# More short products at the start, a new written order of steps, and a split last store in an attention and maxout kernel

## The chip, the cores and the metric

One core of one Trainium2 chip. The metric is the time of one execution on the device in microseconds (us), shown as the median of several runs.

## What is computed

Windowed attention is followed by a maxout feed-forward layer:

```python
scores = scale * np.matmul(q, k.transpose(0, 1, 3, 2))      # 8 batches, 8 heads, 576 positions, 64 wide
attn = softmax(np.where(masks, scores, -1e9))               # window of 32; heads 4 to 7: 128, every 4th position
x = np.matmul(attn, v)                                      # 4608 tokens x 512
h = np.maximum(np.maximum(x @ w1, x @ w2), x @ w3)          # 768 wide
out = h @ w_out                                             # 4608 x 512
```

All data are 32-bit floats. A product of 32-bit operands is made as three products of operands split into a high and a low part.

## The kernel before

Heads are taken two at a time, so a batch has four pairs. The first eight pairs (`early`, L601) are done one by one with small products: scores (L641 adds the mask by an identity product, L649 multiplies q and k), maximum, subtraction, exponential, sum, reciprocal, scaling and a transpose on DVE, ACT and POOL, and then the values (L760). The result of a pair is copied from PSUM as a high part and as a remainder into `xs` (L456, L488); it is one of the four chunks that the first up products (`ups`, L1542) sum over. Tokens go through the layer in tiles of 512, 512, 768, 768, 1024 and 1024. The first two (`plain`, L1534) use plain products of 512 columns (L1551, down products L1490). The four later ones (`fast`, L1625) use a scheme of seven products on sums of blocks (L1793), with sums of the weights that are written to DRAM early (`sums_of`, L1104, stores L1145) and streamed back (L1753); their down products are L1357 (`turned_down`, L1241), whose results leave by `store` (L1376).

Each weight block (`weight`, L512) is loaded (L569), taken apart by ACT (L549), POOL or DVE (L554) and DVE (L560), copied (L456) and its remainder is formed (L488). The 18 blocks of up weights are numbered 0 to 17; step 6j is the load of block j.

Every piece of work is a step of a `Plan` (L275) with a number. The step says what it does and what it depends on, but the order is written out by hand: `SEQUENCE` (L60) lists all step numbers, and `issue` (L311) issues them in this order; each engine therefore runs its own steps in the order of the list and waits at each for what it needs. A letter behind a number (`382d`) names another engine than the step's first choice (a ACT, d DVE, p POOL). `f` is a filler (L2015): one unread bf16 product of 512 columns that only keeps PE busy. Ahead of the list, `issue` calls `short` (L2024) `SHORT` times: an unread product of 32 columns on a 32x32 corner. The first 36 loads are also held back so that no more than 2 million bytes are on their way at once (`gate`, L325).

Numbers that the prediction uses: loads of q and k 152 (pair 2), 170 (pair 0), 188 and 189 (pair 1), 207 (pair 3); loads of v 153, 171, 190, 208 for pairs 2, 0, 1, 3; scores 154, 172, 191, 209 and values 163, 181, 200, 218 for pairs 2, 0, 1, 3; 199 is the transpose for 200; 168 is one copy of pair 2's result; 182, 184, 186 copy pair 0's; 21 and 22 are the DVE and the ACT step of weight block 3; 366, 367, 382, 383 form sums of weight blocks (`both`, L1114).

Of the kernel before, what the change touches and what calls it, by code (L numbers as in the profile page):

```python
# [55 lines left out]
SHORT = 10  # L56
# [278 lines left out]
def tile_dilated_window_attention__then__maxout_ffn(  # L335
# [905 lines left out]
    def turned_down(t0, done, n, hf, load):  # L1241
# [147 lines left out]
        def copied(name, tag, bank, st):  # L1389
            t = buf(tag, name)  # L1390
            return t, plan.add(
                {"act": act(n), "dve": dve(n)}, lambda e: copy(e, t.t[:, :n], bank.t[:, :n]), [st], [bank, t]
            )
# [707 lines left out]
```

## Time and profile before

| | us |
|---|---|
| median of 3 runs | 629.5 (627.93 to 630.55) |
| profiled execution | 629.65 |
| its span, first to last instruction | 627.9 |
| PE busy | 618.7 (99%) |
| DVE busy | 499.4 (80%) |
| ACT busy | 311.9 (50%) |
| POOL busy | 203.0 (32%) |

PE multiplies, DVE, ACT and POOL work on vectors, SP issues loads and stores. The profile's own execution took 1.75 us more than its span. Busy times include the pipeline of a product, so a busy PE need not be PE at its peak; fillers count as busy.

### The profile page before, as it was taken

Reading aid. Unit: us, or ns where it says so; the run is one execution under the profiler, and the core shown is the slowest. Engines: PE = TensorE matmul, PEld = TensorE weight load, DVE = VectorE, ACT = ScalarE, POOL = GpSimd, SP = SyncE. Lnnn points to the kernel's source line nnn. Section 1 sums busy time; section 2 is a strip of 40 time slices with the busy share of each in tenths; the row PEclk is TensorE's granted clock in tenths of the full one; section 3 lists DMA queues with packets and bytes.
Section 4 is the critical chain, followed back from the end, with each engine's and each line's share of the span. In section 5 each row is a group of like instructions: output and inputs, shape, how many; then the busy total and the mean of one; then the engine's idle time right before and its main releaser. Section 6 shows DMA issues by size and latency. Waiting matters only on the chain.

```text
span 627.9 us, 16042 instructions
## 1 busy us (share of the span) xinstructions
PE 618.7 (99%) x6023; PEld 530.4 (84%) x6023; DVE 499.4 (80%) x1385; ACT 311.9 (50%) x932; POOL 203.0 (32%) x252
## 2 busy tenths in 40 slices
PE   9899999999999999999999999999999999999997
PEld 4577887888889999999999999887888888888886
DVE  6878798998899899999989899887759962335665
ACT  3445568575677464776245467822215522122243
POOL 3767988899857512212103010120000000000000
PEclk9899999999999999999999999999999999999999
DMA  7989948987698998878878966477457256757524
GB/s 276 307 282 339 405 149 290 320 286 247 226 348 262 304 301 294 306 253 277 285 244 261 325 226 219 142 230 250 135 184 248 92 170 222 237 178 235 175 84 151
DMA packets 79709, 153.23 MB, mean 244 GB/s; under 512 B 7952, under 2 KB 26384, under 8 KB 79632
## 3 DMA queue, kind: packets, MB, share of 16 engines
q1 hardware_dynamic: 79488, 151.94, 72.0%
q8 instruction: 48, 0.79, 0.5%
q14 instruction: 29, 0.24, 0.1%
q10 hardware_dynamic: 144, 0.26, 0.1%
HBM read 123.08 MB, written 29.10 MB: 242 GB/s over the span
## 4 chain that ended last, share of the span: by engine, by line
PE 88%; DMA 6%; DVE 3%; POOL 1%; ACT 1%; issue 1%; SPq 0%; DVEq 0%; ACTq 0%
PE ffn L1793 47%; PE ffn L1357 16%; PE ffn L1551 13%; PE ffn L1490 3%; PE pair L922 3%; PE pair L1082 3%; PE ffn L2016 1%; DMA kept_up<-hf 1%; DMA wup_a<-kept_up 1%; DMA fk<-in_qk_d_dram 1%; DMA hf<-in_fv_d_dram 1%; DMA kept_d<-dc 1%; DMA st<-in_w_up_dram 1%; DVE hf L488 1%; PE pair L760 1%
## 5 line engine op out<-in xcount | busy, mean ns | idle before, releaser
L1793 PE MATMUL ffn<-wup_a 128*128 128x384 f32 (+1 forms) x1188 | 235.6, 356 | 0.6 <-ACT u L456 0.4
L1793 PEld LDWEIGHTS ffn<-wup_a 128*128 128x128 f32 x1188 | 211.7, 188 | 19.5 <-issue 0.7
L1551 PE MATMUL ffn<-xs,wup_a 128*128 128x512 f32 x408 | 96.7, 394 | 1.5 <-DVE hf L488 1.1
L1551 PEld LDWEIGHTS ffn<-xs,wup_a 128*128 128x128 f32 x408 | 75.6, 188 | 18.6 <-issue 1.5
L488 DVE TENSOR_TENSOR hf<-ffn,hf 128x512 f32<-128x512 f32 (+1 forms) x96 | 60.9, 636 | 36.6 <-PE ffn L1793 33.8
L1026 DVE STREAM_TRANSPOSE PT<-W 32x256 f32<-32x256 f32 (+2 forms) x192 | 76.9, 401 | 4.1 <-POOL sm L996 0.4
L972 ACT ACTIVATE W<-W,mx 128x96 f32<-128x96 f32 (+2 forms) x180 | 65.7, 367 | 10.2 <-DVE mx L960 9.9
L456 ACT CAST hs_all<-hf 128x384 fp32r<-128x384 f32 (+4 forms) x57 | 32.8, 582 | 36.8 <-PE ffn L1357 18.1
L996 POOL TENSOR_SCALAR sm<-sm 128x8 f32<-128x8 f32 (+2 forms) x48 | 11.2, 233 | 121.0 <-ACT W L972 81.2
L456 ACT COPY ffn<-ffn 128x384 f32<-128x384 f32 (+1 forms) x31 | 16.0, 517 | 67.3 <-DVE hf L488 38.7
L1357 PE MATMUL ffn<-hs_all,wdn 128*128 128x512 f32 (+1 forms) x228 | 48.8, 363 | 0.0
L1793 PE MATMUL ffn<-wup_a,wdn 128*128 128x512 f32 x192 | 45.9, 390 | 0.0
L1357 PEld LDWEIGHTS ffn<-hs_all,wdn 128*128 128x128 f32 x228 | 41.3, 188 | 4.8
L456 ACT COPY u<-ffn 128x384 f32<-128x384 f32 (+1 forms) x34 | 18.0, 529 | 52.5 <-PE ffn L1793 46.6
L488 POOL TENSOR_TENSOR W<-W,sm 128x768 f32<-128x768 f32 (+2 forms) x33 | 34.6, 1051 | 25.4 <-DVE sm L1001 24.2
L1793 PEld LDWEIGHTS ffn<-wup_a,wdn 128*128 128x128 f32 x192 | 35.9, 188 | 7.7 <-issue 0.3
L1357 PE MATMUL ffn<-hs_all,wup_a 128*128 128x384 f32 (+1 forms) x198 | 38.8, 350 | 0.0
L488 DVE TENSOR_TENSOR hs_all<-hf,hs_all 128x384 fp32r<-128x384 f32 (+3 forms) x56 | 36.0, 651 | 2.0 <-POOL hs_all L458 1.0
L1357 PEld LDWEIGHTS ffn<-hs_all,wup_a 128*128 128x128 f32 x198 | 35.0, 188 | 2.6 <-POOL hs_all L458 0.2
L458 POOL TENSOR_SCALAR later<-hf 128x512 fp32r<-128x512 f32 x1 | 0.6, 622 | 112.9 <-DVE hf L488 112.9
L960 DVE CUSTOM_DVE_ANT_0 W<-pair,steps 128x96 f32<-128x96 f32 (+1 forms) x158 | 34.5, 250 | 1.9 <-PE pair L922 1.1
L1490 PE MATMUL ffn<-wdn,hs_all 128*128 128x512 f32 x144 | 35.0, 395 | 0.0
(205 smaller groups left out, 1035.3 us busy)
## 6 DMA issues: line engine op xcount, KB each, us to landing
wup_a<-kept_up SPq DMA_DIRECT2D x198, 256.0 KB, 4.3
st<-in_w_up_dram SPq DMA_DIRECT2D x18, 512.0 KB, 5.4
kept_up<-hf SPq DMA_DIRECT2D x36, 256.0 KB, 4.1
wup_a<-kept_d SPq DMA_DIRECT2D x36, 256.0 KB, 4.6
wdn<-kept_up SPq DMA_DIRECT2D x32, 256.0 KB, 3.4
k<-in_qk_d_dram SPq DMA_DIRECT2D x12, 648.0 KB, 6.4
k<-in_qk_p_dram SPq DMA_DIRECT2D x12, 592.0 KB, 5.3
later<-kept_up SPq DMA_DIRECT2D x22, 256.0 KB, 4.2
```

The costliest lines, as they stand in the source:

```text
L456: nc.scalar.copy(dst, src)
L488: (nc.vector if eng == "dve" else nc.gpsimd).tensor_tensor(dst, a, b, op=op)
L922: nc.tensor.matmul(banks[j].t[o : o + nq, 96 * m : 96 * m + nk], kb.t[d, q0 : q0 + nq], kb.t[d, k0 : k0 + nk], start=True, stop=True,)
L960: nc.vector.tensor_tensor_reduce(W.t[rows, a], banks[j].t[rows, 96 * m : 96 * m + nk], mask_of(m)[rows], -0.125, 3e38, ALU.add, ALU.min, m ...
L972: nc.scalar.activation(W.t[rows, a], W.t[rows, a], AF.Exp, bias=mx.t[rows, n : n + 1], scale=-1.0, accum_out=sm.t[rows, n : n + 1],)
L996: nc.gpsimd.tensor_scalar(d, d, 1.0, 1e-9, ALU.mult, ALU.add)
L1026: plan.add({"dve": dve(32 * n) + 0.02}, lambda _: nc.vector.transpose(dst(), src()), [*deps, blank], [W, PT])
L1082: nc.tensor.matmul(pv[z].t[64 * j : 64 * j + 64, q : q + c1 - c0], v.t[d, j, y], PT.t[d, 576 * j + 96 * x + c0 : 576 * j + 96 * x + c1], s ...
L1357: nc.tensor.matmul(bank[e].t[:, :n], weights(wz, e), hop.t[:, hz], start=opens and not q and not m, stop=q == nq - 1 and m == 2, skip_grou ...
L1490: nc.tensor.matmul(bank.t.rearrange("p (k n) -> p k n", k=2), hb.t[:, hz, f], wdn[f].t[:, :, wz], start=(f == 0 and m == 0), stop=(f == NF ...
L1551: nc.tensor.matmul(bank.t, wup[j][:, c // 2, wz, 128 * (c % 2) : 128 * (c % 2) + 128], xs[xz][:, c, first : first + n], start=(m == 0 and ...
L1793: nc.tensor.matmul(bank.t[:, :n], wb.t[:, w : w + 128], xop(o, n)[:, xz, c], start=start and not m and not c, stop=m == 2 and c == 1, skip ...
```

## The change

`SHORT` goes from 10 to 80. `SEQUENCE` is replaced by another order of the same steps (3120 numbers and 45 fillers before, 3122 and 27 after; the two more are those of the split store). The last of the four results of the last tile, until now one copy of 512 columns on ACT and one store that ACT issues, becomes two halves: ACT copies 256 columns and issues their store, DVE copies the other 256 and SP issues their store. `SLOTS` (which buffer each step uses) is unchanged.

```diff
-SHORT = 10
+SHORT = 80
...
 SEQUENCE = (
-    "152 f 170 f 188 f f f 150 f f f f 0 154 189 f 207 155 172 156 f f 157 173 f f 2 f 6 1 f 174 f f f 158 f 175 12 "
-    "191 3 159 160 176 161 f f 153 f 192 f 171 f f 177 f 193 f 8 7 f 138 f 162 f 194 f 4p f f 9 209 151 18 178 195 10 "
-    "179 11 24 163 14 180 13 208 5 f 210 144 f 164 f 168 f 166 f 211 196 f 165 212 169 20 190 167 181 197 19 213 21 "
-    "214 66 f 215 f 15 22 216 f f 538 182 f 186 23 234 25 183 26 184 217 16 225 235 198 236 54 187 239 237 27 218 17 "
-    "185 199 30 238 228 366 219d 223 243 221 220 244 224 245 248 200 42 367 28p 227 36 247 205d 203 229 201d 29 226 "
...
-    "78 63 274 379 68 544 64 276 126 59 65 277 275 67 561 545 73 278 74 381 546 69 96 547 280 279 539 102 75 562 281 "
...
+    "152 188 170 f f f f f f 0 f 154 6 189 155 172 156 1 2 207 f 157 153 f 173 f f 150 8 174 18 158 175 191 3 159 160 "
+    "176 7 161 f f 4 f 9 f f f 177 192 f 12 10 151 f 171 178 193 179 208 11 194 209 162 24 180 f f 163 210 14 13 30 "
+    "195 20 211 f 144 f 164 196 f 166 5 168d 212 165 190 169 138 167 181 213 19 197 214 21 f f 182 215 15 f 22 216 184 "
+    "183 186 538 23 25 225 234 26 60 236 217 16 226 237 198 227 187 239 48 27 218 17 185 199 235 238 223 219d 32 243 "
+    "221 220 228 28 224 248 244 367d 557 200 29 222 31 36 246 366 229 205 201d 247 203d 230 206 204 245 202 249 251 42 "
...
```

In the old list `382d` (DVE) stands behind `543`; in the new one `382`, on POOL, stands behind `275`. The split at the end:

```diff
                     if last and e:
-                        t, st = copied(f"dc{t0}_{e}", "tmp", top[e], prev)
-                        store(1, 0, e, t, [st], by="act")
+                        t = buf("tmp", f"dc{t0}_{e}")
+                        for by, a, z, way in (("act", 0, n // 2, act), ("sp", n // 2, n, dve)):
+                            st = plan.add(
+                                {way.__name__: way(n // 2)},
+                                lambda x, a=a, z=z: copy(x, t.t[:, a:z], top[e].t[:, a:z]),
+                                [prev],
+                                [top[e], t],
+                            )
+                            store(1, 0, e, t, [st], a, z, by)
```

## Rows read from the trace of the kernel before

**Rows 1.** The page: busy time, share of the span and instructions of each engine.

```profile
PE 618.7 (99%) x6023; PEld 530.4 (84%) x6023; DVE 499.4 (80%) x1385; ACT 311.9 (50%) x932; POOL 203.0 (32%) x252
```

**Rows 2.** Windows: length, busy PE, PEld, DVE, ACT, POOL, PEclk, DMA share, GB/s.

```profile
6.87:28.53 21.66, 18.93 (x535) 11.28 (x535) 19.09 (x34) 9.72 (x20) 12.90 (x20) 0.92 0.89 295
...
48.72:624.21 575.49, 574.74 (x5076) 501.72 (x5076) 462.43 (x1314) 291.02 (x893) 173.78 (x205) 1.00 0.72 241
0.98:48.72 47.74, 43.92 (x948) 28.69 (x948) 36.91 (x71) 20.09 (x38) 28.83 (x42) 0.96 0.88 294
```

**Rows 3.** Windows with the fillers (L2016) alone: busy PE, PEld, PEclk, DMA.

```profile
0.98:5.37 4.39, 4.01 (x9) 1.19 (x9) 1.00 0.80 293
...
19.84:22.58 2.74, 2.74 (x6) 0.73 (x6) 0.50 0.85 283
```

**Rows 4.** The waits of PE: us in total, times, longest.

```profile
PE ffn L760 <- DMA hf<-in_fv_d_dram: 1.6, 1, 1.6
PE ffn L1551 <- DVE hf L488: 1.1, 1, 1.1
...
PE pair L649 <- issue: 0.7, 1, 0.7
```

**Rows 5.** The timeline of PE: start, us, instruction, in brackets idle time before.

```profile
0.98 0.44 PE L2026 MATMUL ffn<-raw 32*32 32x32 bf16 x10 [0.98 <-DVE raw L360]
1.35 4.02 PE L2016 MATMUL ffn<-raw 128*128 128x512 bf16 x9
5.17 0.71 PE L641 MATMUL pair<-raw 128*128 128x320 bf16 x2
...
6.99 0.43 PE L641 MATMUL pair<-raw 128*128 128x320 bf16 x2
...
16.68 0.42 PE L649 MATMUL pair<-fk 64*32 64x64 f32 x21 [0.65 <-issue]
...
30.70 2.33 PE L1551 MATMUL ffn<-xs,wup_a 128*128 128x512 f32 x9
...
48.72 9.35 PE L1551 MATMUL ffn<-xs,wup_a 128*128 128x512 f32 x40 [1.09 <-DVE hf L488]
```

**Rows 6.** The chain that ended last: start, us, what.

```profile
6.87 6.33 DMA fk<-in_qk_d_dram
...
13.21 5.38 DMA hf<-in_fv_d_dram
...
28.31 4.97 DMA st<-in_w_up_dram
```

**Rows 7.** The timeline of DVE in the first 50 us.

```profile
6.87 0.82 DVE L677 TENSOR_REDUCE fmx<-pair 128x10 f32<-128x640 f32 x1 [1.91 <-PE pair L649]
...
13.77 0.83 DVE L741 STREAM_TRANSPOSE PT<-W 128x640 f32<-128x640 f32 x1
...
18.30 0.79 DVE L677 TENSOR_REDUCE fmx<-pair 128x10 f32<-128x640 f32 x1
19.11 0.82 DVE L488 TENSOR_TENSOR hf<-pair,fmx 128x640 f32<-128x640 f32 x1
...
25.60 0.39 DVE L488 TENSOR_TENSOR xs<-pair,xs 128x256 fp32r<-128x256 f32 x1
...
27.70 0.83 DVE L741 STREAM_TRANSPOSE PT<-W 128x640 f32<-128x640 f32 x1
...
47.28 0.69 DVE L488 TENSOR_TENSOR hf<-wup_a 128x512 f32<-128x512 f32 x1 [1.92 <-DMA kept_up<-hf]
```

**Rows 8.** The weight loads of the short products (PEld) in the timeline.

```profile
0.98 0.33 PEld L2026 LDWEIGHTS <-raw 32*32 32x32 bf16 x10 [0.98 <-DVE raw L360]
```

**Rows 9.** The page: DMA queue, packets, MB, share of 16 engines.

```profile
q8 instruction: 48, 0.79, 0.5%
```

**Rows 10.** The timeline of the last 4 us.

```profile
624.25 0.59 ACT L456 COPY dc<-ffn 128x512 f32<-128x512 f32 x1 [1.45 <-PE ffn L1357]
624.87 0.37 ACTq L1381 DMA_DIRECT2D out_dram<-dc  x1
```

258 rows, old and new, of the table SEQUENCE are left out of this document.

## The prediction

> **What bounds the kernel now.** I read the page first. PE is busy for 618.7 of 627.9 us and DVE for 80% [rows 1], so the kernel is bound by PE, and only what PE does besides real products can be won. The windows say where that is. From 48.72 us to the end of the last product at 624.21 us PE is busy for 574.74 of 575.49 us [rows 2]: 0.75 us of idle time in nine tenths of the kernel. A new order of the steps there can win no more than this; it can lose more. From 0.98 to 48.72 us PE shows 43.92 us of 47.74 as busy [rows 2], but part of that is unread work: 10 short products and 45 fillers, of which the first nine alone take 4.01 us [rows 3]. All that the change can win, save the tail, lies in these 48 us.
>
> The list of PE's waits then names the idle times [rows 4]: 1.6 us for a load of v, 1.1 us for DVE in the up products, 0.7 us called "issue" (nothing that the profile shows). The timeline places the last two before 48.72 and 16.68 us [rows 5]. The chain runs in the first 19 us through two loads, 6.33 us for the q and k of pair 3 and then 5.38 us for the v of pair 2 [rows 6]. But a shorter chain of loads isn't yet an earlier start of dense products, because DVE stands behind it: from the first maximum at 6.87 us to the end of step 199's transpose at 28.53 us (27.70 + 0.83) it is busy for 19.09 of 21.66 us [rows 2, 7]. That is the bound I go by.
>
> **The change part by part.** *The short products.* Ten of them start at 0.98 us and the first filler at 1.35 us, 0.037 us each [rows 5], so 70 more take 2.6 us of PE time; by their weight loads, 0.33 us for ten [rows 8], it is 2.3 us. Two fillers fewer stand ahead of the first scores (7 for 9), which gives back 2 x 4.01 / 9 = 0.9 us [rows 3]. So the first scores begin 1.4 to 1.7 us later. Nothing hides this: DVE has been idle for 1.91 us when it gets just these scores [rows 7]. The clock can soften it. PE ran the first nine fillers at the lower level (512 columns in 0.446 us is 1.2 GHz) and two products of 320 columns in 0.43 us at 6.99 us, at the higher one, after 0.71 us at 5.17 us [rows 5]. If it rises at the same moment in the new kernel, the last one or two of the seven fillers cost half, 0.2 us each, and the delay is 1.0 us. I take 1.2 us, between 0.9 and 1.7.
>
> *The instruction packets.* What the short products may bring is that PE gets through the first part of its program earlier, so that the next packet is fetched earlier. The row that bears on it is an idle 0.65 us inside the fourth scores, before 16.68 us, ended by nothing that the profile shows [rows 5]; 48 packets hold 0.79 MB, 16.4 KB each [rows 9]. So at most 0.65 us, once. And the reader of these scores, DVE, came to them only at 18.30 us [rows 7], over a microsecond after they were done, which makes it worth nothing: I take 0, with 0.65 us kept as the end. The Trainium skill (Runtime: NRT & Kernel Launch, Instruction fetch mechanics) says that blocks of 16 KiB are fetched while the current one runs and that crossing a boundary is mostly hidden; by that rule the gain is 0 and the 70 products are a pure cost. The packet size agrees with the row; whether the 0.65 us is such a packet no row shows.
>
> *The order of the loads.* The v of pair 2 (153) now stands right behind 207 and no longer behind two weight blocks as well, so it can be issued soon after the first scores free the buffer of 207, at some 8 us and not at 13.21 us [rows 6]. The 1.6 us wait for it goes. Late next is DVE: pair 2's transpose, done at 14.6 us now [rows 7], has 9, 193 and 11 ahead of it besides the 1.2 us, and comes at some 17 us. Values of pair 2 gain a microsecond or two by this, but it is not yet dense work, because the up products need all four chunks. Weight block 5 (30), the load that ends the chain's stretch of 28.31 to 33.28 us [rows 6], moves from the twentieth load to the fourteenth and is out of the way.
>
> *The dense start.* DVE's work up to step 199 is the same set in both orders, plus copy 168 that comes from ACT, 0.4 us by a 256-column piece [rows 7]. With no gap it ends at 6.87 + 1.2 + 19.09 + 0.4 = 27.6 us; with all the gaps of now (21.66 - 19.09 = 2.57 us) at 30.1 us. I take half the gaps, 28.9 us for 28.53. The values that read it (200) end at 30.70 us now, 2.2 us later, since up products stand ahead of them [rows 5]; in the new order they come straight behind 199 and take some 1.2 us, with one up product more (0.23 us) done before, 13 for 12. Dense work is then at 28.9 + 1.2 - 0.2 = 29.9 for 30.7: -0.8, with ends of -2.3 and +0.9 (the later first scores among them).
>
> *The wait at 48.72 us.* DVE stood 1.92 us behind a store of weight sums until 47.28 us [rows 7], in step 382; the maximum queued behind it held a bank of PE's, 1.09 us of idle PE [rows 5]. In the new order 382 is POOL's; DVE takes 367 in exchange (0.7 us, early). I take -0.8 of the 1.09 us. The end on the other side is 0, if POOL waits for the same store and the weight blocks queued behind 382 on POOL are late in its place.
>
> *Fillers.* 18 fewer; two are counted above, the rest stood in time in which PE had nothing to do. They cost nothing by themselves. What would cost is a clock that falls: at 19.84 us six fillers took 2.74 us at a granted clock of 0.50 (1.2 GHz), after the 1.6 us wait [rows 3, 4].
>
> *The tail.* The last copy takes 0.59 us for 512 columns [rows 10]; the longer half is DVE's, 0.4 us by its 256-column row [rows 7]. The two stores carry the same bytes as the one. I take -0.2 us, between 0 and -0.4 (if a shorter transfer ends earlier, too).
>
> *After 48.72 us.* 0, between -0.75 and +1.6 (one more wait as long as the longest now [rows 4]).
>
> **Sum**, on the profiled execution's 629.65 us (0.15 above the median): -0.8 - 0.8 - 0.2 = -1.8, so 627.9 us. About 0.5%, 3.15 us, is what a measurement of this kernel can tell from no change: the forecast lies within it.
>
> **The rivals.** *The front closes up.* DVE runs without gaps (-2.3), the wait goes in full (-1.09), and the tail gives 0.4: 629.65 - 3.8 = 625.9 us; with the later idle time gone too, 625.1. For it: the gaps are there, and the loads come in a better order. Against it: an engine in order that three others feed has seldom no gap, and all terms must come at their ends.
>
> *Only the short products count.* DVE keeps its gaps (+0.9), the wait at 48.72 us only changes its place, the tail gives 0.2: 630.4 us. For it: the packet's 0.65 us held up nobody. Against it: 382 has left DVE.
>
> *Slower: ACT holds pair 0's copies.* In the new list ACT has 182, then 22 (weight block 3's copy, which needs DVE's 21), then 184 and 186. The fifth up product needs 186. DVE's 18 steps up to 211 took from 6.87 to 19.93 us [rows 7], 13.1 us; with half the gaps 12.3 us, so they end at 20.4 us. The four pieces of pair 2 (0.4 us each), 213 (0.8), 197 (0.2) and 21 (0.7) end at 23.7 us, and 22, 184 and 186 behind them (0.6, 0.4, 0.4) at 25.1 us. The first four up products are done by 22.2 us: 3 us in which PE does nothing but wait. If the clock falls as in [rows 3], the nine up products and pair 3's values that stand before 200, 3.1 us, take up to 6.2 us and end at 31.3 us, where 28.9 us was wanted. 200 and what follows is 2.4 us late against the sum above, and the first dense products run at the lower level for another 3 us, 1.5 us lost: 627.9 + 2.4 + 1.5 + 0.8 (the wait at 48.72 us comes back, since DVE is late with PE) = 632.6 us, and with DVE's gaps kept 633.5 us. It decides from the point where the clock falls; at the higher level the wait is swallowed by the slack before 200, and nothing is lost.
>
> **How the numbers follow.** Forecast near 627.9 (626.4 to 629.5): 0.46. Closed front: 0.26. Only the short products: 0.14. Slower, about 633: 0.14. Faster by over 0.5% is below 626.35, the closed front: 0.26. Slower by over 0.5% is above 632.65: 0.14. Within: 0.60. The range for 8 in 10 takes in the forecast, the third case and the closed front down to 624.8 (cheaper short products), and ends at 631.3, without the slower case.
>
> **What would show it.** Right: first scores at 6.3 to 6.9 us; the 1.6 us wait for v gone; the fourth transpose ended between 28 and 30 us; no wait of PE at 48 us; PE idle below 1 us after that; an end copy of 0.4 us. Wrong: dense up products well before 28 us (then DVE was not the bound), a granted clock of 0.5 between 22 and 31 us (the slower case), or new waits in the hundreds of us that follow.

## The result: slower, and the profile after

The new kernel takes 635.48 us (median of 9 runs, 631.34 to 637.3), the old one beside it 629.39 us: a ratio of 1.0087, 95% interval 1.0061 to 1.0112, or 5.5 us more. The profiled execution of after took 633.95 us, below its median; its span is 632.1 us, 4.2 us over that of before. Its last product ends at 628.56 us, 4.35 us later than before's 624.21, so the difference lies with PE. These two executions are the ones that the traces explain; the medians lie further apart than they do. The windows split that time, by the stretch's length, PE's busy time in it, and the busy time of the lines of fillers and short products alone:

| us, from 0.98 to the last product's end | before | after | change |
|---|---|---|---|
| idle (length less busy) | 4.58 | 9.92 | +5.34 |
| fillers (45, then 27) | 13.93 | 9.56 | -4.37 |
| short products (10, then 80) | 0.44 | 2.31 | +1.87 |
| all other products | 604.28 | 605.79 | +1.51 |

A filler does no work either, so idle time and fillers belong together: 18.51 us before, 19.48 after, +0.97. Most of the new idle time stands where fillers stood; the 4.35 us are these 0.97, the 1.87 of the short products and the 1.51 of the other products.

The windows of after answer to [rows 2]; columns are length, busy PE, PEld, DVE, ACT, POOL, PEclk, DMA share, GB/s:

```profile
0.98:48.87 47.89, 37.97 (x971) 25.41 (x971) 31.56 (x62) 18.06 (x35) 22.69 (x35) 0.89 0.84 280
48.87:628.56 579.69, 579.69 (x5110) 507.34 (x5104) 463.50 (x1319) 295.05 (x901) 180.76 (x211) 1.00 0.72 240
```

All 9.92 us of idle time stand before 48.87 us; behind it PE has none, where it had 0.75 us. PE's waits, for [rows 4]:

```profile
PE ffn L760 <- issue: 3.7, 1, 3.7
PE pair L649 <- issue: 3.3, 2, 1.7
PE pair L760 <- issue: 2.2, 1, 2.2
PE ffn L2033 <- DVE raw L360: 1.0, 1, 1.0
PE pair L760 <- DVE c L560: 0.6, 1, 0.6
```

The 1.6 us for v and the 1.1 us for DVE are gone. In their place stand 9.2 us in four pieces called "issue", which waits for nothing that the profile shows. PE's timeline gives their places:

```profile
10.78 0.45 PE L649 MATMUL pair<-fk 64*32 64x64 f32 x28 [1.59 <-issue]
...
17.45 0.99 PE L649 MATMUL pair<-fk 64*32 64x64 f32 x76 [1.68 <-issue]
...
23.43 0.35 PE L760 MATMUL ffn<-PT,hf 32*64 32x48 f32 x4 [3.74 <-issue]
...
30.54 0.27 PE L760 MATMUL pair<-PT,hf 32*64 32x64 f32 x2 [0.57 <-DVE c L560]
...
36.64 0.71 PE L760 MATMUL pair<-PT,hf 32*64 32x64 f32 x43 [2.23 <-issue]
37.28 6.66 PE L1558 MATMUL ffn<-xs,wup_a 128*128 128x512 f32 x21
```

What they have in common shows when the products between them are counted (windows of PE; x is the count; the columns behind it are PEclk, DMA share, GB/s):

```profile
0.90:9.50 8.60, 8.21 (x223) 1.00 0.88 312
10.70:16.50 5.80, 4.99 (x128) 1.00 0.90 294
17.40:21.00 3.60, 2.24 (x127) 1.00 1.01 348
23.40:30.20 6.80, 6.54 (x128) 0.65 0.87 300
30.50:36.00 5.50, 3.76 (x127) 1.00 0.94 301
```

PE stops after 223 products and then after each 128 (127 where waits for semaphores stand among them: the trace has exactly 256 instructions of PE, weight loads, matmuls and such waits, from each of these points to the next). A product is a weight load and a matmul, so 128 products are 256 instructions; the queue "instruction" moved 48 packets of 16.4 KB for 6075 products, about 127 each. Before's one such idle time fits: windows of before count 351 = 223 + 128 products up to 16.3 us, where PE stood for 0.65 us [rows 5]. Narrow windows of the DMA view find packets starting at 8.5, 15.2, 21.2, 28.2 and 34.3 us, and PE goes on 2.2 to 2.4 us after each. So the 0.57 us that the list puts down to DVE may be the same thing, as it stands on the fourth of these points; the DVE step ended 0.1 us before PE went on, too, so which of the two held it isn't told.

These are waits for the program, and not only here: in the 20 traces of this case all 54 idle times of PE that are called "issue" and last 0.15 us or more stand at such a point, 223 products and a multiple of 256 instructions. The Trainium skill (Runtime: NRT & Kernel Launch, Instruction fetch mechanics) calls the crossing of a boundary mostly hidden; behind 49 us that holds in this run, and in the front, where 127 small products kept PE busy for only 2.24 us from 17.4 us on, it does not: up to 3.74 us stood open.

What the waits did is seen at the dense start, the first product behind the values of step 200: 30.70 us in before [rows 5], 37.28 us in after, 6.6 us later. From there to the last product (windows of PE in before, then in after):

```profile
30.70:624.21 593.51, 591.67 (x5306) 1.00 0.72 243
37.28:628.56 591.28, 591.28 (x5304) 1.00 0.72 240
```

The new kernel needs 2.2 us less there, 1.84 of it idle time that is gone. All that it loses, and more, it loses before the dense start.

The clock fell as well. Up to the dense start the products that are neither fillers nor short take 14.51 us in after and 12.61 in before, 0.23 of the difference for one up product more; the granted clock is 0.50 in after from 21.4 to 28.1 us, in before from 19.4 to 22.7 us. It falls once more behind the last stall. Twenty-one up products there, windows of their line in after (the column ahead of the last two is PEclk):

```profile
37.28:43.90 6.62, 6.62 (x21) 5.00 (x21) 0.74 0.67 242
```

and twenty-eight of the same shape in before:

```profile
40.95:47.60 6.65, 6.65 (x28) 5.18 (x28) 1.00 0.81 247
```

PE had stood for 2.23 us shortly ahead of the first. The granted clock of 0.74 is a mixture of the two levels, 1.2 and 2.4 GHz; at before's rate the 21 products take 5.0 us, so 1.6 us went there. The stretch from the dense start on isn't longer for it as a whole (591.28 us busy for 591.67); where the 1.6 us came back isn't shown.

### The profile page after: what moved, and what is told of

Read it like the earlier page. It is cut to its first block, busy times and chain, and to the rows that moved or that the text cites. A ratio compares the mean times of both kernels' runs of the same rounds, so it can differ in the third digit from the quotient of the medians.

```text
span 632.1 us, 16173 instructions
## 1 busy us (share of the span) xinstructions
PE 617.7 (98%) x6075; PEld 532.8 (84%) x6075; DVE 495.6 (78%) x1383; ACT 313.7 (50%) x936; POOL 203.9 (32%) x251
## 4 chain that ended last, share of the span: by engine, by line
PE 96%; issue 2%; DVE 1%; POOL 0%; ACT 0%; POOLq 0%
PE ffn L1800 48%; PE ffn L1357 16%; PE ffn L1558 16%; PE ffn L1497 5%; PE pair L922 3%; PE pair L1082 3%; PE pair L649 1%; PE ffn L2023 1%; PE pair L760 1%; PE ffn L1082 1%; PE ffn L760 0%; PE pair L641 0%; DVE xs L488 0%; PE ffn L2033 0%; POOL hf L488 0%
## 5 line engine op out<-in xcount | busy, mean ns | idle before, releaser
L1558 PE MATMUL ffn<-xs,wup_a 128*128 128x512 f32 x408 | 98.0, 398 | 0.0
L456 ACT COPY ffn<-ffn 128x512 f32<-128x512 f32 (+1 forms) x34 | 17.7, 520 | 94.4 <-DVE hf L488 48.2
L996 POOL TENSOR_SCALAR sm<-sm 128x8 f32<-128x8 f32 (+2 forms) x48 | 13.9, 289 | 123.6 <-ACT W L972 91.6
L456 ACT CAST hs_all<-hf 128x384 fp32r<-128x384 f32 (+4 forms) x56 | 32.1, 580 | 28.2 <-PE ffn L1357 16.9
L458 POOL TENSOR_SCALAR hs_all<-hf 128x384 fp32r<-128x384 f32 (+3 forms) x5 | 3.6, 718 | 112.6 <-DVE hs_all L488 110.9
L488 DVE TENSOR_TENSOR hs_all<-hf,hs_all 128x384 fp32r<-128x384 f32 (+2 forms) x55 | 35.4, 648 | 4.1 <-ACT hs_all L456 3.5
L456 ACT COPY hf<-ffn 128x512 f32<-128x512 f32 (+1 forms) x35 | 19.3, 551 | 34.5 <-PE ffn L1800 20.8
```

Source lines behind the costliest of these rows:

```text
L456: nc.scalar.copy(dst, src)
L488: (nc.vector if eng == "dve" else nc.gpsimd).tensor_tensor(dst, a, b, op=op)
L996: nc.gpsimd.tensor_scalar(d, d, 1.0, 1e-9, ALU.mult, ALU.add)
L1558: nc.tensor.matmul(bank.t, wup[j][:, c // 2, wz, 128 * (c % 2) : 128 * (c % 2) + 128], xs[xz][:, c, first : first + n], start=(m == 0 and ...
```

## Experiments

"Old" and "new" are the two lists of steps. Ratios are to the old kernel in the same set of runs, with 95% intervals. Ledgers are as in the table above.

**The short products apart from the order.** `new_short10`: the new kernel with

```diff
-SHORT = 80
+SHORT = 10
```

> The new kernel with 10 short products for 80; order and tail stay new. Theory A (program packets): PE's program comes in packets of 128 products, the third and later ones at a pace of their own (resumed at 10.78, 17.45, 23.43, 36.64 us in the new kernel, at the products 223, 351, 479, 735), and 70 products more at the start use them up earlier. With 10, product 223 lies in the third scores and the 1.59 us stall at 9.2 us is gone; the idle time called issue falls from 9.2 us to 2 to 6 us; time 629.5 to 632.5 us. Theory B (the new order itself loses the time, through loads and the ACT and DVE queues): 634 to 636 us, as with 80. Theory C (only the 2.3 us that the short products take): 633 us, with the same stalls.

633.08 us, 1.0066 (1.0043 to 1.009). The stall in the second scores is gone and "issue" is 2.7 us, but PE stands 2.64 us for a load, idle time is 9.24 us (3.33 of it behind 50 us) and all other products take 606.77 us: granted clock 0.52 at 25 to 30 us. A's stall is gone as it said and its time is not met: with 10 short products the new order still loses 4.1 us (2.7 to 5.7). Its ratio isn't told apart from the 1.0087 (1.0061 to 1.0112) with 80, so how much of the 5.5 us the short products cost in the new list isn't shown.

`old_short80`: the old kernel with

```diff
-SHORT = 10
+SHORT = 80
```

> The old kernel with 80 short products; order and tail stay old. Theory A: product 223 now lies in the second scores and 351 in the fillers ahead of the fourth, so PE stands there until its packets come, near 10.8 and 17 us; issue waits of 3 to 8 us for 0.65, time 632 to 636 us, and a wider spread from run to run. Theory B: only the 2 us of the short products, most of them covered by fillers: 629.5 to 631.5 us. Theory C: 631.5 us, issue wait unchanged.

635.9 us, 1.0115 (1.0092 to 1.0139): the time that A says, 7.2 us for 70 short products that take 1.9 us. In the old list their cost is shown. The places are not A's: packets came at 6.35 and 11.33 us here, PE passed product 223 and 351 without a stop and stood at later boundaries (18.95, 24.17, 38.03 and 106.19 us). PE's waits:

```profile
PE ffn L760 <- issue: 2.2, 2, 1.7
PE pair L649 <- issue: 1.9, 1, 1.9
PE pair L760 <- issue: 1.8, 1, 1.8
```

The last stands at 106 us, among the values of a later pair: a moved boundary can cost late, too.

**Time or count?** `new_fill5` starts the first scores as late as the new kernel, with 65 products fewer ahead of them:

```diff
-SHORT = 80
+SHORT = 10
...
-    "152 188 170 f f f f f f 0 f 154
+    "152 188 170 f f f f f f f f f f f 0 f 154
```

> The new kernel with 10 short products and 5 more fillers in the place of the 70 others: the first scores begin as late as in the new kernel (6.2 us), but only 5 products and not 70 are ahead of the list. Theory A: stalls as with 10 short products, so the same time as that run to 1 us (630 to 633 us). Theory C (the delay of the first scores costs): as the new kernel, 634 to 636 us. Theory B: 634 to 636 us.

631.76 us, 1.0053 (1.0037 to 1.0069), against 1.0087 (1.0061 to 1.0112) with the short products. It lies in A's range and 2 us under C's, so the delay isn't the main cost; the two intervals just overlap, and from the 1.0066 of `new_short10` it isn't told apart. The packets still came late (0.87, 2.0 and 2.3 us of "issue").

**The same products late.** `old_late70` leaves 10 at the start and puts 70 ahead of weight block 9; PE makes them from 60.35 to 62.26 us:

```diff
+            if st is self.steps[288] or st is self.steps[292]:
+                if st.bufs[0].slot == 7:
+                    for _ in range(70):
+                        short()
             x = st.fn(eng)
```

> The old kernel with 10 short products at the start, and the other 70 in front of the up products of weight block 9, near 55 us, where PE works on 512-column products and its program is ahead of it. Every packet boundary behind that point lies where it lay with 80 at the start. Theory A (short products cost where PE outruns its program, in the first 45 us): only their own time, 70 x 0.027 = 1.9 us, to 2.4 us: 630 to 631.5 us. Theory V (the boundaries moved behind 50 us cost, the old list with 80 having 4.07 us of idle time there): 633 to 636 us.

632.54 us, 1.0048 (1.0026 to 1.0071): +3.0 us (1.6 to 4.5) for a busy time of the short products of 2.35 us, 1.9 over before. The time lies between A's range (missed by 1.0 us) and V's (missed by 0.5), so a part of V holds: PE stood 1.55 us for program at 103.90 us, on the boundary that `old_short80` shows at 106 us. But the same products late cost less than half of what they cost at the start, and of the 7.2 us there some 4 are the front's.

**More of them.** `new_short160`:

```diff
-SHORT = 80
+SHORT = 160
```

> The new kernel with 160 short products for 80. Theory A: packets come one by one, the next asked for only when PE enters the one before, so what counts is the number of products in front of the dense ones: 80 more are five eighths of a packet at some 6 us a packet, of which the earlier first request gives back up to 3 us. First packet's transfer starts at 4.5 to 6.5 us for 8.47; stalls of 8 to 12 us; time 635.5 to 640 us. Theory E (packets come at times of their own, whatever PE has used up): first transfer at 8 to 9 us, and 80 products more use them up sooner: over 641 us. Theory F (early short products do help the packets on, and 80 were too few): below 634 us.

630.34 us, 1.0044 (1.0023 to 1.0065), against 1.0087 (1.0061 to 1.0112): 80 more short products make the new kernel faster. Theory A as written here falls, and F holds. The first packet's transfer starts between 6.8 and 7 us for 8.5 us, and the idle time is 4.39 us for 9.92. An earlier request fits this, with a gain far above the "up to 3 us" against five eighths of a packet; that it is the cause, and not the boundaries that now fall at other products, isn't shown.

`new_short138` and `new_short208` move every boundary by one whole packet against 10 and 80:

```diff
-SHORT = 80
+SHORT = 138
```

> The new kernel with 138 short products: 10 and one packet. Theory P: as with 10, 632 to 634.5 us. Theory L: as with 160, 629.5 to 631.5 us.

632.14 us, 1.0047 (1.0023 to 1.007): in P's range, but by its ratio not told apart from either 10 or 160.

```diff
-SHORT = 80
+SHORT = 208
```

> The new kernel with 208 short products: 80 and one packet. The first scores begin 3.7 us later than with 80. Theory P: the boundaries lie as with 80, the issue waits are as there (about 9 us), time 635 to 639 us. Theory L: the first request is as early as with 160, waits of 2 to 4 us, time 630.5 to 633 us, 1.4 us of it for 48 products more than 160.

633.48 us, 1.0071 (1.0045 to 1.0097), idle time 5.43 us. The time is neither theory's, 0.5 us above L's range and 1.5 under P's; the waits called "issue" are 3.4 us, as L said (2 to 4), and not about 9.

`old_short160` and `old_short0`, the old kernel with

```diff
-SHORT = 10
+SHORT = 160
```

> The old kernel with 160 short products, all fillers kept. The first scores begin some 4 us later than now. Theory L: the packets are ahead of PE, so only the later start counts, part of it covered: 628.5 to 631 us, far below the 635.9 us with 80. Theory N: above 637 us. Theory P: the boundaries lie as with 32 short products, between the 628.3 us with 10 and the 635.9 us with 80.

634.65 us (631.18 to 640.72), 1.0075 (1.0053 to 1.0098): in P's range, above L's and below N's, with 5.06 us of idle time behind 50 us in its profile.

```diff
-SHORT = 10
+SHORT = 0
```

> The old kernel without short products. Theory A as a dose (80 cost 7.5 us more than 10, and each fewer helps): 626.8 to 628.2 us. Theory W (the old list is fitted to the boundaries that it has with 10, and any shift costs): 629.5 to 633 us.

629.38 us, 1.0006 (0.9982 to 1.003): above A's range, and no loss as W had it; ten fewer change nothing that can be told.

**Short products in the place of fillers.** `old_short147_no_fill`:

```diff
-SHORT = 10
+SHORT = 147
...
-    "152 f 170 f 188 f f f 150 f f f f 0 154
+    "152 170 188 150 0 154
```

> The old kernel with 147 short products for 10 and without the nine fillers ahead of the first scores: 128 products more, so every packet boundary lies where it lay in the old kernel, one packet later, and the first scores begin as early (147 x 0.0286 = 4.2 us for 0.4 + 4.0). Theory L (lead: whole packets of unread products at the start let PE ask for its first packet at 3 to 4 us for 6.5, and all later ones are earlier): transfers of the first packets 2 to 3 us earlier, the idle 0.65 us gone, 626.5 to 628.3 us. Theory P (only where the boundaries lie matters): as the old kernel, 628 to 629 us. Theory N (each packet more in the front costs its 5 to 6 us): 632 to 635 us. A clock that the short products do not raise would show as granted clock or filler-like products at 0.43 us in the first scores.

632.82 us, 1.0062 (1.0035 to 1.0088): L and P fall here, and the number is N's, but for a reason of its own. PE's timeline:

```profile
0.98 4.10 PE L2026 MATMUL ffn<-raw 32*32 32x32 bf16 x147 [0.98 <-DVE raw L360]
5.02 0.71 PE L641 MATMUL pair<-raw 128*128 128x320 bf16 x2
...
8.99 0.41 PE L649 MATMUL pair<-fk 64*16 64x64 f32 x6 [1.99 <-issue]
...
11.74 3.92 PE L2016 MATMUL ffn<-raw 128*128 128x512 bf16 x10
```

The ten fillers at 11.74 us take 0.39 us each, most of them 0.43 us, which is the 1.2 GHz level, where ten at 8.32 us took 0.23 us each in before. (The level is read from the durations: the granted clock of a window reads 1.00 here, as it does for before's first fillers of 0.446 us [rows 3].) So 4.1 us of 32-column products have not raised the clock. PE also stood for 1.99 us in between, but `new_short208`, which has no such stop, shows the same; its seven fillers take 0.45 us each behind 5.7 us of short products:

```profile
0.98 5.73 PE L2033 MATMUL ffn<-raw 32*32 32x32 bf16 x208 [0.98 <-DVE raw L360]
6.64 3.17 PE L2023 MATMUL ffn<-raw 128*128 128x512 bf16 x7
```

And at 74 products into the first scores of `old_short147_no_fill` PE ran out of program (147 + 2 + 74 = 223).

**Loads and packets.** `new_ahead1`:

```diff
-GATED, AHEAD = 36, 2e6
+GATED, AHEAD = 36, 1e6
```

> The new kernel with at most 1 million bytes of early loads on their way for 2 million. Theory G (a packet is late because it queues behind the loads): the transfer of a packet starts 2 to 3 us after PE enters the packet before, for 3.7 to 4.8 us now (10.78 to 15.18, 17.45 to 21.19, 23.43 to 28.22), and issue waits fall below 6 us for 9.2; the time falls by 1 to 3 us if the loads are not later in turn. Theory H (a fixed time): 3.7 to 4.8 us as now, issue waits as now, time the same or up to 3 us longer by later loads.

666.98 us, 1.0613 (1.0591 to 1.0636), with 33.8 us of idle time: the loads are far too late. Both G and H fall, by something not thought of. PE's timeline:

```profile
9.69 0.45 PE L649 MATMUL pair<-fk 64*32 64x64 f32 x28 [0.72 <-issue]
10.07 1.04 PE L2023 MATMUL ffn<-raw 128*128 128x512 bf16 x4
10.94 0.43 PE L641 MATMUL pair<-raw 128*128 128x320 bf16 x2
15.94 1.39 PE L649 MATMUL pair<-hf 64*32 64x64 f32 x80 [4.56 <-DMA hf<-in_qk_p_dram]
```

At 9.69 us PE enters a packet, does 28 + 4 + 2 = 34 products of it and stands for a load. Windows of 2 us from 10 to 18 us hold no transfer of program; the next one starts at 18.4 us, 2.5 us after PE has gone on. The same trace shows it a second time: PE stands 2.97 us until 28.35 us, and the next packet starts at 30.8 us, again 2.5 us later. In these two cases a PE that stood early in a packet did not get the next one meanwhile: the wait for data and the wait for program came one behind the other. The first packet did start earlier than in the new kernel, at 7.4 us for 8.5, with a first stop of 0.72 us for 1.59; whether the fewer loads did that, one execution of each doesn't tell.

**What the new order loses.** `new_q_first` exchanges two loads, `new_fill10_third` puts unread work into the wait for them (both with 10 short products):

```diff
-0 f 154 6 189 155
+0 f 154 189 6 155
```

> The new list with 10 short products and the second half of pair 1's q and k (189) loaded ahead of weight block 1 (6), as in the old list, instead of behind it. Theory Q (this load is what the new front loses: with 10 short products PE stood 2.64 us for it at 12.37 us, the clock fell, and the first packet came late too, since PE does not ask for the next while it stands): the wait is below 0.8 us, the time outside waits, fillers and short products falls from 606.8 to 605 us, 629.5 to 631.5 us. Theory R (the next load, 207, or the packets take its place): 632 to 634 us.

633.17 us, 1.0076 (1.0048 to 1.0104): the wait fell from 2.64 to 0.4 us and the time did not. R holds; "issue" took its place (3.9 us, 2.0 of them at 107 us).

```diff
-158 f 175 191
+158 f 175 f f f f f f f f f f 191
```

> The new list with 10 short products and 10 more fillers ahead of the third scores, where PE stood 2.64 us for the load. Theory K (a wait that PE spends in unread products costs less than one that it spends standing, since the clock stays up and PE gets on in its program): idle time in the first 50 us down by 2 to 3 us, granted clock near 1 at 10 to 15 us, the rest of PE's time from 606.8 to below 605.5 us; 630 to 632 us. Theory R: 632.5 to 634.5 us, the fillers' 2.2 us replacing the wait and nothing else.

631.99 us, 1.0064 (1.0036 to 1.0092). Granted clock 1.0 up to 15 us as K says, but then 2.6 us of "issue" in the fourth scores and a clock of 0.5 from 20 to 30 us. The time lies at the end of K's range, but the ratio is that of `new_short10` (1.0066): K's gain is not there. With 160 short products the exchange of the loads (`new_q_first_160`) gave 631.0 us, 1.0035 (1.0006 to 1.0064), not told apart from the 1.0044 without it:

> The same exchange with 160 short products, the best count for the new list so far (630.3 us). There the third scores come later than the load, so theory Q and R both expect nothing from it: 629.5 to 631.5 us; if below 629 us it is the version to keep.

The other three put one list in front of the other, with 10 short products. `old_front` has the old list up to step 276, near 47 us, `new_front` the new one up to there, `old_front_long` the old one up to step 1180, near 190 us; the rest follows in the other order. The first lines of the lists in `old_front`:

```diff
 SEQUENCE = (
-    "152 188 170 f f f f f f 0 f 154 6 189 155 172 156 1 2 207 f 157 153 f 173 f f 150 8 174 18 158 175 191 3 159 160 "
...
+    "152 f 170 f 188 f f f 150 f f f f 0 154 189 f 207 155 172 156 f f 157 173 f f 2 f 6 1 f 174 f f f 158 f 175 "
...
```

> 10 short products; the old list up to step 276 (the up products of weight block 6, near 47 us), then all other steps in the order of the new list; split tail. Theory A (what the new order loses, it loses in the first 50 us, where packets, loads and the small products of the first pairs meet): as the old kernel, 627.5 to 629.5 us. Theory D (the new order also loses later, in waits for streamed blocks and packets that fall into the later score products): 630 to 632 us.

631.79 us (629.51 to 635.65), 1.0069 (1.0034 to 1.0103): D.

> 10 short products; the new list up to step 276, then all other steps in the order of the old list; split tail. Theory A: as the new kernel with 10 short products, 631.5 to 634 us, with its 2.6 us wait for the q of pair 1 and a granted clock near 0.5 around 25 us. Theory D: between, 629.5 to 631 us.

631.79 us, 1.0063 (1.0035 to 1.0091): A by its median, its wait (2.40 us for the q of pair 1) and its clock (0.50 from 22.9 to 29.7 us); the interval reaches into D's range.

> 10 short products; the old list up to the first product of the tile that starts near 190 us, then the new order; split tail. The old list up to 47 us alone gave 631.8 us (629.5 to 635.7). Theory S (what is lost behind 47 us is lost up to 190 us, where small products and packets still meet): 627.5 to 629.5 us, as the old kernel. Theory D (lost in waits for streamed blocks after 190 us): 630 to 632.5 us.

628.99 us, 1.0 (0.9976 to 1.0023): S. Behind 190 us the new order loses nothing that can be told. Before it, either half of it is enough to lose 4 us, and both together (`new_short10`) lose no more.

**The tail.** `old_two_tiles`, the old kernel with the split store alone, and a tile for each half:

```diff
-                        t, st = copied(f"dc{t0}_{e}", "tmp", top[e], prev)
-                        store(1, 0, e, t, [st], by="act")
+                        for by, a, z, way in (("act", 0, n // 2, act), ("sp", n // 2, n, dve)):
+                            t = buf("tmp", f"dc{t0}_{e}_{by}")
...
```

> The old kernel with the split last store alone, and each half in a tile of its own. In the new kernel DVE's half began only when ACT's had ended (28.60 + 0.37, then 0.42 us), 0.8 us in all for the 0.59 us of the one copy. Theory T1: the shared tile orders the two halves; with two tiles both start at once and the copies end 0.4 us after the last product, 0.2 us before now. Theory T2: it is the bank that both read, and DVE still starts behind ACT. Either way the time is that of before within 0.3 us.

628.49 us, 1.0003 (0.9988 to 1.0017). Its timeline shows T2:

```profile
621.63 0.37 ACT L456 COPY dc_act<-ffn 128x256 f32<-128x256 f32 x1 [1.45 <-PE ffn L1357]
622.03 0.37 ACTq L1381 DMA_DIRECT2D out_dram<-dc_act  x1
622.04 0.42 DVE L460 COPY dc_sp<-ffn 128x256 f32<-128x256 f32 x1 [3.25 <-ACT dc_act L456]
```

DVE starts when ACT has ended though the tiles that they write differ. What they still share is the tile, and with it the bank, that both read; whether the chip or the program orders them there isn't shown.

## Why the prediction was wrong

The forecast was 1.8 us less than before; it came 5.5 us more.

*The step that failed* is the one on the instruction packets. It took the one idle 0.65 us for all that packets could cost, "at most 0.65 us, once", and took 0, as a gain that nobody needed. The new kernel's trace has 9.24 us in four waits for program in its place, 0.57 us more that may be one, and the dense start, forecast at 29.9 us, came at 37.28. The sign was wrong as well, at least in the old list: 70 more products at the start cost 7.2 us there, since every later boundary moves with them. The rows to see it were there: the one stop [rows 5], 351 products into the program by the windows above, and 48 packets for 6023 products [rows 1, 9], about 125 each, from which the next boundaries could have been looked for among the small products of the new list. The rule of the Trainium skill (Runtime: NRT & Kernel Launch, Instruction fetch mechanics), that the crossing is mostly hidden, stood beside a row that spoke against it.

This step is not the whole of the loss. With 10 short products "issue" is 2.7 us and the new order loses 4.1 us all the same; the forecast's sum had no term for that, but had named its price under *Fillers*, a clock that falls.

*The short products* themselves were nearly right: 2.31 us for 80, first scores at 6.19 us for a forecast of 6.3 to 6.9, 1.0 us later for 1.2, first maximum at 8.17 us for 6.87 + 1.2 = 8.07 us. That the last one or two fillers would cost half did not come true (seven in 3.17 us).

*The order of the loads* was right as far as it went: the v of pair 2 is issued at 9.50 us for 13.21, and the wait for it is gone, though PE stood for program until 17.45 us. *The dense start* was mis-sized. DVE in after:

```profile
8.17 0.82 DVE L677 TENSOR_REDUCE fmx<-pair 128x10 f32<-128x640 f32 x1 [3.19 <-PE pair L649]
...
31.75 0.83 DVE L741 STREAM_TRANSPOSE PT<-W 128x640 f32<-128x640 f32 x1
```

Its work up to step 199 is 19.04 us, as the 19.09 us of [rows 2] said, but the transpose ends at 32.58 us and not at 28.9: the gaps are 24.41 - 19.04 = 5.37 us for 1.3 forecast and 2.57 before. DVE was not what set the end. Nearly all of its gaps are waits for PE, 1.48 us for the second scores, 2.67 and 1.09 us for values, and the first two of these PE had made late for want of program. And step 200 itself then stood for 2.23 us. The -0.8 us became +6.6 (37.28 for 30.70 us).

*The wait at 48.72 us* is gone, as forecast (that step 382's move did it isn't shown apart), and nothing followed: no idle time behind 48.87 us. *Fillers* were taken to cost nothing, with a falling clock as the only price; this price was paid (granted clock 0.63 and 0.69 in 20 to 25 and 25 to 30 us), 1.5 us net on other products. As fillers shrank by 4.37 us, idle time grew by 5.34. *The tail* gave no more than 0.1 us for 0.2: some 3.6 us from the last product to the end of the span in both, since the halves follow one another (0.37 + 0.42 us for 0.59).

*The rivals.* The slower one had the size (633 us) and the falling clock, but not the cause: no wait of PE on ACT's copies is in the list. "Only the short products count" named them and gave them the wrong price, 630.4 us.

*What stays open.* Why the new order is slower with the old count of short products. The ledgers go one step: in the five profiles with the new list's front and 10 short products (`new_short10`, `new_fill5`, `new_q_first`, `new_fill10_third`, `new_front`) idle time and fillers are 17.5 to 19.5 us, as in before (18.5), but other products take 606.5 to 607.4 us for 604.3, and the granted clock from 5 to 50 us is 0.89 to 0.92 for 0.96. So 2 to 3 of the 4 us go with the lower clock; that it is all of the difference isn't shown. Which wait lets it fall isn't told apart, either: with the load of q out of the way it fell all the same. `old_front` doesn't fit this: its fastest execution, the only profiled one, has 604.28 us of other products and shows no loss.

And why the count of short products works so unevenly (new list: ratios of 1.0066, 1.0087, 1.0047, 1.0044 and 1.0071 for 10, 80, 138, 160 and 208; most of these are not told apart from each other). Packet boundaries that fall here or there among small products fit this; that they are the whole of it is argued, not shown. No version here is told to be faster than the old kernel.

## What to carry to other kernels

Count instructions as well as time where many small ones run: a filler, a short product or a reordering moves every later boundary of the program's packets, and a packet that is late shows as idle time that ends on nothing, at the same count of instructions each time. Unread work of the same length isn't the same work: 512-column fillers used few instructions and let the clock rise, 32-column products used many and did not. Where one order has been fitted to such waits, test a change of it by the counts between idle times ahead of looking at loads and engines.

## What the hardware showed unexpectedly

PE ran dry after 223 products and after every 256 instructions from there on, some 128 products, when small products ran faster than packets came, and in the new kernel went on 2.2 to 2.4 us after a packet's transfer began; no idle time called "issue" of 0.15 us or more in the 20 traces stands anywhere else. While PE stood at the 34th product of a packet for 4.56 us, the next one was not transferred, and came 2.5 us after PE had gone on. And 147 products of 32 columns in 4.1 us left the clock at its lower level, which most of the next fillers, 0.39 us each on average, still had from 11.74 us on; after 208 of them in 5.7 us it was the same.
